# Reordering the opening loads and the opening TensorE jobs of a fused local-attention and squared-ReLU kernel

## The chip, the cores and the metric

The kernel runs on one core of one Trainium2 chip. The metric is the device time of one execution in microseconds (us); lower is better. A comparison of two kernels is made on medians of several executions.

## The reference, cut to what matters

Attention over 4 batches, 8 heads, 768 positions and 64 channels, with a window of 96 positions behind the query and 8 global positions, a distance penalty for each head, and then a two-layer network with a squared ReLU over the 3072 resulting rows.

```python
scores = scale * np.matmul(q, k.transpose(0, 1, 3, 2))
keep = is_global | is_local
scores = np.where(keep, scores - slopes[:, None, None] * dist, -1e9)
a = softmax(scores)
x = np.matmul(a, v)          # -> 3072 rows of 512
h = np.maximum(x @ w_in, 0.0)          # 512 -> 2048
out = h * h @ w_out                    # 2048 -> 512
```

## The kernel before, in words

**Tiling.** A batch has six tiles of 128 rows; a *half* is three tiles, so there are eight halves (`halves[0]` to `halves[7]`, called x0, x1, ...). A query tile meets two key blocks: its own tile, and the block before it, in which the global keys replace the first 32 rows (`kb` for keys, `vb` for values). All work on a half is: load q, k, v; turn q and k so that the 64 channels lie on the partitions; scores; exponentials; weights times v; division by the row sum; turn the result into `xt`; first layer with `w_in_sb`; ReLU and square into `h2`; second layer with `w_out_sb`; store.

**Two regimes.** From the third half on, the attention of the next half is merged into the two dense layers of the present one, so TensorE has always dense work between the small matmuls. The first two halves (batch 0) have no dense work to hide behind. They are handled tile by tile by an *opening*: a list of job names written out by hand, `OPENING`. Its jobs are:

- `T r`: eight TensorE transposes of q and k of tile r (`turn_tile`), two copies out of PSUM, and for inner tiles the `kb` copies.
- `S r o`, `S r b`: scores of tile r with its own block, or with the block before (`score_tile`). For tiles 0 to 2 the distance penalty is added by eight more matmuls; for tiles 3 to 5 the exponentials are multiplied by a mask on VectorE. Two exponentials on ScalarE follow each.
- `V r`: the copies for `vb` (`fix_v`). `A r i`: weights times v for four heads (`attend_tile`), then reciprocal and product on VectorE (`norm`). `X r i`: two transposes into `xt` (`tile_to_x`).
- `F c`, `G c i`: first layer of x0 with quarter c of `w_in`, for tile 0 and for tiles 1 and 2. `E c i`, `D c`: the same for x1, tiles 3 and 4, and tile 5.

After the opening come the rest of the first layer of x1, and the second layer of x0, whose first matmul (line 606) marks the end of the opening in the trace.

**What sets the order.** The program is recorded by a class `Plan`. TensorE jobs stand in one queue and loads in another, each in the order in which they were listed; all other operations are picked by the plan's own costs and due times. The plan then emits everything in that order, and each engine runs its queue strictly in order. Where the plan sees TensorE idle early on, it fills with matmuls on zeros (`warm`, lines 207 and 210), half as many as the idle time holds in the first 5 us. PSUM is given out in rings: `big` has six buffers (transposes of q and k, scores, layers), `att` two (weights times v, and the transposes into `xt`).

**Loads.** All q, k, v tiles but the first q and k, and all weights, are issued by GpSimd (`plan.load`, line 95), which converts fp32 to fp16 on the way. q and k of tile 0 come as fp32 through SyncE and ScalarE (`rsq`, `rsk`, line 330) and are converted by copies. Before any load GpSimd fills two index tables (`fill_index`, lines 227 and 229), on which the identity `ident` (line 233), the mask and all warm transposes rest. The loads were listed as: k1 q1 v0, k2 q2 v1, v2; two quarters of `w_in`; k3 q3 v3, k4 q4 v4, k5 q5 v5; two quarters of `w_in`; four quarters of `w_out`.

Of the kernel before, what the change touches and what calls it, by code (L numbers as in the profile page):

```python
# [8 lines left out]
FP32 = mybir.dt.float32  # L9
# [4 lines left out]
P = 128  # L14
# [2 lines left out]

OPENING = """T0 T1 S0o S1o A00 T2 A01 S1b S2o X01 X00 S2b A10 V1 A11 F0 A20 V2 X10 F1 A21 X20 T3 X11 V3  # L20
X21 S3b S3o T4 G10 G00 T5 S4b A31 A30 S4o G01 G11 G21 X31 S5b A40 G20 X30 S5o A41 V4 G31 G30
X41 X40 F3 A50 A51 E10 F2 E01 X51 E11 X50 E00 D0 D1"""


class Op:
    def __init__(self, costs, emit, needs, rank=0, lag=0.0, land=None, slots=()):
        self.costs, self.emit, self.rank, self.lag, self.land = costs, emit, rank, lag, land
        self.needs = [n for n in needs if n is not None]
        self.slots = slots
        self.done = None  # L30
        self.wait = 0.0
# [17 lines left out]
class Plan:  # L49
# [10 lines left out]
    def __init__(self, warm_from, warm_until):  # L60
        self.warm_from, self.warm_until = warm_from, warm_until
        self.queues = {"PE": [], "LOAD": []}
        self.rest = []
        self.free = {}
        self.landed = 4.4
        self.rank = 0

    def pe(self, cost, emit, needs=(), takes=(), lag=0.24):
# [23 lines left out]
        self.rest.append(op)  # L92
        return op

    def load(self, dur, emit, needs=(), rank=None):
        rank = self.rank + 0.5 if rank is None else rank
        op = Op({"POOL": 0.88}, emit, needs, rank, 0.7, land=dur)
        self.queues["LOAD"].append(op)
        return op

# [8 lines left out]
    def run(self):  # L109
        order = []  # L110
        while self.rest or any(self.queues.values()):
            best = None
            for op in [q[0] for q in self.queues.values() if q] + self.rest:
                r = self.ready(op)
                if r is None:
                    continue
                e = min(op.costs, key=lambda e: max(r, self.free.get(e, 0.0)) + op.costs[e])
                c = (max(r, self.free.get(e, 0.0)), op.rank, e, op)
                if best is None or c[:2] < best[:2]:
                    best = c  # L120
            start, _, e, op = best
            end = start + op.costs[e]
            idle = self.free.get(e, self.warm_from)
            self.free[e] = end
            op.done = end + op.lag
            if op.land is not None:
                self.landed = max(end + 0.8, self.landed) + op.land
                op.done = self.landed + op.lag
            for q in self.queues.values():
                if q and q[0] is op:  # L130
                    q.pop(0)
                    break
            else:
                self.rest.remove(op)
            self.spare = 0.0
            if e == "PE" and start < self.warm_until and op.users:
                self.spare = start - 0.1 - max([idle] + [n.done for n in op.frees])
                self.spare *= 0.5 if start < self.warm_from + 5.0 else 1.0
            op.emit(e)
            order.append((start, end, e, op))  # L140
        return order
# [3 lines left out]
def kernel(  # L145
# [11 lines left out]
    nc = tc.nc  # L157

    B, H, S, D = q.shape
# [7 lines left out]
    HT = HALF // P  # L167
# [9 lines left out]
    stage_p = ctx.enter_context(tc.tile_pool(name="stage", bufs=2))  # L177
# [8 lines left out]
    plan = Plan(1.0, 24.0)  # L186
# [5 lines left out]
    def copy(e, out, in_):  # L192
        if e == "ACT":
            nc.scalar.copy(out=out, in_=in_)  # L194
        else:
            eng(e).tensor_copy(out=out, in_=in_)  # L196
# [24 lines left out]
    w_in_sb = const.tile([P, NCT, d_ff], FP16, name="w_in_sb")  # L221
# [51 lines left out]
    batches = [Batch() for _ in range(B)]  # L273
    halves = [Half() for _ in range(NHB)]
    for hb, x in enumerate(halves):
        x.hb, x.b, x.half = hb, hb // 2, hb % 2
        x.bt = batches[x.b]
    w_in_op, w_out_op = [], []

    def new_batch(bt):  # L280
        bt.qk = qk_p.tile([P, 2, NT, NPAIR, P], FP16, name="qk", tag="qk")
# [9 lines left out]
    def staged(x, name):  # L291
        if getattr(x, name, None) is None:
            setattr(x, name, stage_p.tile([P, HT, H, D], FP16, name=name, tag=name))
        return getattr(x, name)

    def list_loads(x):
        r0 = x.half * HALF
        prev = halves[x.hb - 2] if x.hb >= 2 else None
        before = (prev.turned if prev else []) + (halves[x.hb - 1].turned if x.hb > 3 else [])
        vbefore = [halves[x.hb - x.half - 3].attended[-1]] if x.hb >= 4 else []  # L300

        def rows(src, name, t):
            def emit(e):
                dst = (x.bt.v[:, x.half * HT + t, :, 0:D] if name == "v"
                       else staged(x, name)[:, t, :, :])
                dma = nc.gpsimd.dma_start(out=dst, in_=src[x.b, :, r0 + t * P:r0 + (t + 1) * P, :]  # L306
                                          .rearrange("h p d -> p h d"))
                if x.hb > 3 and name == "sq" and t == 0:
                    for turn in halves[x.hb - 1].turns:
                        behind(dma, turn)  # L310
                if name == "sk":
                    x.last_load = dma
            return plan.load(0.85, emit, vbefore if name == "v" else before)

        if x.half == 0:
            def start(e):
                new_batch(x.bt)
                nc.vector.memset(x.bt.v[:, :, :, D:D + 1], 1.0)
            x.bt.op = plan.add({"DVE": 0.1}, start, vbefore, rank=0)
        if x.hb > 1:  # L320
            x.q_in = [rows(q, "sq", t) for t in range(HT)]
            x.k_in = [rows(k, "sk", t) for t in range(HT)]
            x.v_in = [rows(v, "v", t) for t in range(HT)]
        elif x.hb == 1:
            x.k_in, x.q_in, x.v_in = zip(*((rows(k, "sk", t), rows(q, "sq", t), rows(v, "v", t))
                                           for t in range(HT)))
        else:
            def first(dst, src, eng, e, lag):
                raw = stage_p.tile([P, H, D], FP32, name="r" + dst, tag="r" + dst, bufs=1)
                op = plan.add({e: 0.5}, lambda e: eng.dma_start(  # L330
                    out=raw, in_=src[0, :, 0:P, :].rearrange("h p d -> p h d")), rank=-1)
                op.lag = lag

                def emit(e):
                    copy(e, staged(x, dst)[:, 0], raw)
                return plan.add({"DVE": 0.42, "ACT": 0.54}, emit, [op], rank=0)
            x.k_in = [first("sk", k, nc.scalar, "ACT", 4.1)]
            x.q_in = [first("sq", q, nc.sync, "SP", 3.4)]
            x.v_in = []
            for t in range(1, HT):  # L340
                x.k_in.append(rows(k, "sk", t))
                x.q_in.append(rows(q, "sq", t))
                x.v_in.append(rows(v, "v", t - 1))
            x.v_in.append(rows(v, "v", HT - 1))
        for l in x.v_in:
            l.needs.append(x.bt.op)
        x.bt.v_in = [*getattr(x.bt, "v_in", []), *x.v_in]

    def list_w_in(cs):
        n = d_ff // 4  # L350
        for c in cs:
            w_in_op.append(plan.load(2.65, lambda e, c=c: nc.gpsimd.dma_start(  # L352
                out=w_in_sb[:, :, c * n:(c + 1) * n],
                in_=moe_w_in[:, c * n:(c + 1) * n].rearrange("(k p) f -> p k f", p=P))))

    def list_w_out():
        n = NFT // 4
        for c in range(4):
            w_out_op.append(plan.load(2.65, lambda e, c=c: nc.gpsimd.dma_start(
                out=w_out_sb[:, c * n:(c + 1) * n, :],  # L360
                in_=moe_w_out[c * n * P:(c + 1) * n * P, :].rearrange("(m p) d -> p m d", p=P))))

# [435 lines left out]
    x0, x1 = halves[0], halves[1]  # L798
    tile_ops, kb_ops, tiles = {}, {}, {}
    for bt in batches:  # L800
# [2 lines left out]
    zero_op = plan.add({"DVE": 0.2}, lambda e: nc.vector.memset(zero, 0.0), rank=-3)  # L803
    index = plan.add({"POOL": 0.5}, fill_index, rank=-2)
    list_loads(x0)
    ident_op = plan.add({"DVE": 0.25}, fill_ident, [index], rank=0)
    dist_op = plan.add({"DVE": 2.4}, fill_dist, [ident_op], rank=0)
    slope_ops = [plan.add({"DVE": 0.2}, fill_dist16, [dist_op], rank=0)]
    slope_ops += [plan.add({"ACT": 0.3, "DVE": 0.18}, lambda e, h=h: fill_slope_id(e, h), [ident_op],
                           rank=0) for h in range(H)]  # L810
    mask_ops = [plan.add({"ACT": 0.43}, lambda e, h=h: fill_mask(h), [dist_op], rank=10 + h)
                for h in range(H)]
    list_w_in((0, 1))
    list_loads(x1)
    list_w_in((2, 3))
    list_w_out()

    jobs = {}
# [8 lines left out]
    for c in range(4):  # L827
# [3 lines left out]
        for i in range(2):  # L831
            jobs[f"G{c}{i}"] = lambda ms=ms, i=i: layer1(x0, ms[2 * i:2 * i + 2], P, HALF)
            jobs[f"E{c}{i}"] = lambda ms=ms, i=i: layer1(x1, ms[2 * i:2 * i + 2], 0, 2 * P)
    for name in OPENING.split():
        jobs[name]()
    for job in l1(x1, 8) + l2(x0)[:6]:
        job()
    for hb in range(1, NHB):
        x = halves[hb]
# [51 lines left out]
```

## Time and profile before

| | us |
|---|---|
| median of 6 runs (lowest to highest) | 221.12 (220.59 to 221.75) |
| the profiled execution | 220.91 |
| its span in the profile | 219.1 |
| TensorE busy in the span | 211.5 (96%) |
| ScalarE busy | 128.0 (58%) |
| VectorE busy | 117.2 (54%) |
| GpSimd busy | 68.2 (31%) |

The span is what the profile covers from the first to the last instruction; 1.8 us of the execution lie around it. Busy time of TensorE includes the matmuls on zeros, and matmuls overlap in the pipeline, so a share of 96% is not 96% useful work. Times inside the trace are counted from the start of the span.

### The profile page before, as it was taken

To read this page: it belongs to the slowest core of one execution; us is meant where nothing else is said; L and a number is where in the kernel's file an instruction comes from. 1 tells how busy PE (TensorE), PEld (TensorE's weight loads), DVE (VectorE), ACT (ScalarE), POOL (GpSimd) and SP (SyncE) were. 2 spreads that over 40 slices of the span, in tenths; PEclk is the share of its full clock that TensorE was granted. 3 is DMA by queue.
4 is the path that set the end of the run, shared out by engine and by line. 5 is a ranking of instruction groups with operands and counts; after the bars stand their busy time and mean duration, and the time that the engine had idled before them with its cause. 6 is when DMAs were issued, how large, how long until landed. Compare 5 with 4: busy or idle time off the path is not lost.

```text
span 219.1 us, 4865 instructions
## 1 busy us (share of the span) xinstructions
PE 211.5 (96%) x1928; PEld 128.5 (59%) x1928; DVE 117.2 (54%) x336; ACT 128.0 (58%) x289; POOL 68.2 (31%) x84
## 2 busy tenths in 40 slices
PE   6989899999999999999999999999999999999993
PEld 6767789855555556445654565446554565455552
DVE  7476788433764298606963388407850479104300
ACT  7796897653753779119841688139831786137421
POOL 8986824485058049003900094000000000000000
PEclk9999999999999999999999999999999999999999
DMA  8999999999989959956994999964103101220012
GB/s 122 148 194 157 188 207 207 163 152 142 167 164 155 206 125 154 159 127 139 129 120 112 212 73 151 117 135 106 39 19 114 52 18 39 66 96 0 3 48 95
DMA packets 106727, 26.41 MB, mean 120 GB/s; under 512 B 99408, under 2 KB 103760, under 8 KB 106704
## 3 DMA queue, kind: packets, MB, share of 16 engines
q0 software_dynamic: 77024, 13.37, 87.5%
q1 hardware_dynamic: 28640, 12.46, 23.5%
q10 hardware_dynamic: 1040, 0.26, 0.6%
q8 instruction: 15, 0.25, 0.5%
q14 instruction: 8, 0.07, 0.1%
HBM read 27.26 MB, written 6.29 MB: 153 GB/s over the span
## 4 chain that ended last, share of the span: by engine, by line
PE 76%; DMA 9%; POOL 9%; DVE 2%; ACT 1%; issue 1%; SPq 0%; POOLq 0%
PE hps L557 35%; PE yps L606 30%; DMA v<-in_v_dram 7%; PE av L502 4%; PE sp L447 3%; POOL sk L306 3%; POOL sq L306 3%; POOL v L306 2%; DMA qk<-sk 2%; PE yps L634 2%; PE av L734 1%; POOL w_in_sb L352 1%; ACT qk L194 1%; ACT ex L462 1%; PE sp L695 1%
## 5 line engine op out<-in xcount | busy, mean ns | idle before, releaser
L557 PE MATMUL hps<-xt,w_in_sb 128*128 128x384 f16 (+2 forms) x608 | 89.3, 301 | 0.0
L606 PE MATMUL yps<-w_out_sb,h 128*128 128x512 f16 x368 | 83.0, 379 | 0.0
L557 PEld LDWEIGHTS <-w_in_sb 128*128 128x128 f16 x608 | 53.7, 98 | 26.8 <-DMA w_in_sb<-in_moe_w_in_dram 0.4
L581 ACT ACTIVATE hr<-hps 128x384 f16<-128x384 f32 (+1 forms) x108 | 55.0, 518 | 16.0 <-PE hps L557 13.5
L592 DVE TENSOR_TENSOR h<-hr 128x768 f16<-128x768 f16 (+1 forms) x70 | 36.1, 522 | 52.0 <-ACT hr L581 51.4
L606 PEld LDWEIGHTS <-h 128*128 128x128 f16 x368 | 35.1, 98 | 39.5
L194 ACT COPY y<-yps 128x512 f32<-128x512 f32 (+1 forms) x25 | 14.3, 570 | 59.5 <-PE yps L606 56.9
L462 ACT ACTIVATE ex<-sp 128x384 f16<-128x384 f32 x96 | 36.7, 476 | 2.2 <-PE sp L447 2.1
L306 POOL DMA_DIRECT2D sq<-in_q_dram x23 | 20.4, 893 | 53.8 <-DMA qk<-sq 30.6
L306 POOL DMA_DIRECT2D sk<-in_k_dram x23 | 20.7, 916 | 7.3 <-DVE ph L716 3.6
L306 POOL DMA_DIRECT2D v<-in_v_dram x24 | 21.6, 929 | 3.4 <-DMA w_out_sb<-in_moe_w_out_dram 3.3
L196 DVE COPY vb<-v 128x520 f16<-128x520 f16 (+1 forms) x32 | 10.1, 321 | 9.7 <-DMA v<-in_v_dram 9.2
L511 DVE TENSOR_TENSOR tm<-av,rec 128x384 f16<-128x384 f32 x24 | 13.4, 557 | 0.8
L196 DVE COPY kb<-qk 128x96 f16<-128x96 f16 (+4 forms) x56 | 11.0, 302 | 5.1 <-ACT qk L194 4.2
L502 PEld LDWEIGHTS <-phat 128*128 128x128 f16 x264 | 10.0, 98 | 3.9 <-DVE phat L478 0.7
L478 DVE TENSOR_TENSOR phat<-ex,mask 128x768 f16<-128x768 f16 x24 | 12.2, 549 | 0.0
L502 PE MATMUL av<-v,phat 128*128 128x65 f16 x168 | 11.5, 194 | 0.1
L509 DVE RECIPROCAL rec<-av 128x6 f32<-128x6 f32 x24 | 4.7, 196 | 12.4 <-PE av L502 12.1
L474 DVE TENSOR_TENSOR phat<-ex,mask 128x768 f16<-128x768 f16 (+1 forms) x24 | 10.6, 485 | 0.1
L502 PE MATMUL av<-vb,phat 128*128 128x65 f16 x96 | 10.2, 194 | 0.3 <-DVE phat L478 0.3
L194 ACT COPY qk<-trp 128x512 f16<-128x512 f16 (+1 forms) x14 | 7.5, 562 | 4.9 <-DVE qk L196 2.7
L447 PE MATMUL sp<-qk 64*128 64x128 f16 x168 | 8.9, 219 | 0.0
(67 smaller groups left out, 138.0 us busy)
## 6 DMA issues: line engine op xcount, KB each, us to landing
out_dram<-y SPq DMA_DIRECT2D x23, 256.0 KB, 2.2
v<-in_v_dram POOLq DMA_DIRECT2D x24, 128.0 KB, 6.6
sk<-in_k_dram POOLq DMA_DIRECT2D x23, 128.0 KB, 5.8
sq<-in_q_dram POOLq DMA_DIRECT2D x23, 128.0 KB, 5.3
w_in_sb<-in_moe_w_in_dram POOLq DMA_DIRECT2D x4, 512.0 KB, 8.5
w_out_sb<-in_moe_w_out_dram POOLq DMA_DIRECT2D x4, 512.0 KB, 14.8
xt<-tm SPq DMA_TRANSPOSE x20, 2.9
rsk<-in_k_dram ACTq DMA_DIRECT2D x1, 256.0 KB, 4.7
```

Of the source, the lines that this page charges most:

```text
L194: nc.scalar.copy(out=out, in_=in_)
L196: eng(e).tensor_copy(out=out, in_=in_)
L306: dma = nc.gpsimd.dma_start(out=dst, in_=src[x.b, :, r0 + t * P:r0 + (t + 1) * P, :] .rearrange("h p d -> p h d"))
L447: nc.tensor.matmul(pair[h][:, i * P:(i + 1) * P], lhsT=lhsT, rhs=bt.qk[rows, 0, r, a, :], start=True, stop=True)
L462: nc.scalar.activation(out=st["ex", g][:, h, 0:n], in_=st[g][h][:, 0:n], func=AF.Exp, scale=scale)
L478: eng(e).tensor_tensor(out=phat[:, :, c0:c0 + n].rearrange("p e (i c) -> p e i c", c=P), in0=ex[:, :, 0:n].rearrange("p e (i c) -> p e i c ...
L502: nc.tensor.matmul(av[:, h, j, :], lhsT=phat[:, h, c * P:(c + 1) * P], rhs=rhs, start=n == 0, stop=n == len(mine) - 1)
L511: nc.vector.tensor_tensor(out=st["tm"].rearrange("p t e d -> p e t d"), in0=av[:, :, :, 0:D], in1=rec[:, :, :, None].to_broadcast([P, 2, H ...
L557: nc.tensor.matmul(st["ps"][:, i * n:(i + 1) * n], lhsT=w_in_sb[:, kk, m * P:(m + 1) * P], rhs=x.xt[:, kk, c0:c1], start=kk == 0, stop=kk ...
L581: nc.scalar.activation(out=o, in_=i, func=AF.Relu)
L592: eng(e).tensor_tensor(out=x.h2[:, m0:m0 + width, c0:c1], in0=hr, in1=hr, op=ALU.mult)
L606: nc.tensor.matmul(st["ps"], lhsT=x.h2[:, m, j * P:(j + 1) * P], rhs=w_out_sb[:, m, :], start=m == 0, stop=m == NFT - 1)
```

## The change

`OPENING` is replaced by another order, and the opening loads get an order of their own, `LOADING`: q and k of tiles 1 to 5 and v of tiles 0 to 2 stand ahead of the first quarter of `w_in`; v3, v4 and v5 stand between and behind the quarters. The first of these loads (k of tile 1) has rank -3, ahead of the index tables (rank -2), so GpSimd issues it first. The rest changes the plan's own costs and due times (they decide what is picked next and how many matmuls on zeros are put in), not the operations. In the built program GpSimd's queue begins: load k1, iota, iota, q1, k2, q2, k3, v0, q3, v1, q4, k4, v2, k5, q5, c0, v3, c1, v4, c2, c3, v5, then four quarters of `w_out` (cN is quarter N of `w_in`). The matmuls on zeros are 40 ahead of T0, 14 ahead of T1, 4 ahead of T2 and 1 later: 59, where there were 36, 18 and 14 more: 68. VectorE converts k of tile 0 and ScalarE q of tile 0; before, VectorE did both. From the second layer of x0 on, TensorE's order is the same.

```diff
-OPENING = """T0 T1 S0o S1o A00 T2 A01 S1b S2o X01 X00 S2b A10 V1 A11 F0 A20 V2 X10 F1 A21 X20 T3 X11 V3
-X21 S3b S3o T4 G10 G00 T5 S4b A31 A30 S4o G01 G11 G21 X31 S5b A40 G20 X30 S5o A41 V4 G31 G30
-X41 X40 F3 A50 A51 E10 F2 E01 X51 E11 X50 E00 D0 D1"""
+OPENING = """T0 T1 S0o T2 S1o S2o A00 A01 S1b X00 S2b T3 V4 A10 A11 S3o V1 T4 A21 X01 S3b X11 V3 A20 X21
+S4o X10 X20 S4b T5 G01 V2 A30 F0 G00 S5b F1 X30 S5o G10 A40 A41 G11 G21 G20 X40 G30 A31 X41
+F3 X31 A51 G31 A50 E11 X51 E10 X50 E00 D0 D1 E01 F2"""
+LOADING = """k1 q1 k2 q2 k3 v0 q3 v1 q4 k4 v2 k5 q5 c0 v3 c1 v4 c2 c3 v5"""
...
-        self.free = {}
-        self.landed = 4.4
+        self.free = {e: 0.75 for e in ("ACT", "DVE", "POOL", "SP")}
+        self.landed = 3.4
...
-    def load(self, dur, emit, needs=(), rank=None):
+    def load(self, dur, emit, needs=(), rank=None, lag=2.6):
         rank = self.rank + 0.5 if rank is None else rank
-        op = Op({"POOL": 0.88}, emit, needs, rank, 0.7, land=dur)
+        op = Op({"POOL": 0.92}, emit, needs, rank, lag, land=dur)
...
-                self.landed = max(end + 0.8, self.landed) + op.land
+                self.landed = max(end + 1.45, self.landed) + op.land
...
+            for t in range(HT):
+                r = x.half * HT + t
+                if r > 0:
+                    for src, name, key, ops in ((k, "sk", "k", x.k_in), (q, "sq", "q", x.q_in)):
+                        load_jobs[f"{key}{r}"] = lambda src=src, name=name, ops=ops, t=t: (
+                            ops.__setitem__(t, rows(src, name, t, -3 if not plan.queues["LOAD"]
+                                                    else None)))
+                load_jobs[f"v{r}"] = lambda t=t: (
+                    x.v_in.__setitem__(t, rows(v, "v", t)), x.v_in[t].needs.append(x.bt.op))
...
     list_loads(x0)
+    list_loads(x1)
+    for c in range(4):
+        load_jobs[f"c{c}"] = lambda c=c: load_w_in(c)
+    x0.k_in[0] = first_tile(x0, "sk", k, nc.scalar, "ACT", 3.8)
+    x0.q_in[0] = first_tile(x0, "sq", q, nc.sync, "SP", 3.4)
+    for name in LOADING.split():
+        load_jobs[name]()
...
-    dist_op = plan.add({"DVE": 2.4}, fill_dist, [ident_op], rank=0)
+    dist_op = plan.add({"DVE": 2.1}, fill_dist, [ident_op], rank=0)
...
-    list_w_in((0, 1))
-    list_loads(x1)
-    list_w_in((2, 3))
     list_w_out()
```

## The prediction, made before the changed kernel ran

> **What bounds the kernel now.** I read the clock and span first, then the busy time by stretches, the waits, TensorE's timeline of the opening, and the transfers. The stretches (time, TensorE busy, weight loads, VectorE, ScalarE, GpSimd, clock, share of the DMA engines, GB/s):
>
> ```profile
> 0.00:5.50 5.50, 3.83 (x36) 3.83 (x36) 4.04 (x17) 4.24 (x12) 4.74 (x11) 1.00 0.85 122
> 5.50:8.50 3.00, 2.73 (x37) 2.44 (x36) 1.28 (x2) 1.81 (x6) 3.00 (x4) 1.00 2.35 149
> 8.50:16.00 7.50, 6.62 (x124) 5.29 (x121) 5.00 (x15) 6.90 (x16) 6.66 (x9) 1.00 1.54 179
> 16.00:25.00 9.00, 8.06 (x121) 6.27 (x118) 5.70 (x21) 6.25 (x14) 6.38 (x9) 1.00 2.25 163
> 25.00:47.00 22.00, 22.00 (x277) 18.14 (x278) 15.81 (x47) 17.89 (x36) 10.70 (x14) 1.00 1.66 188
> ```
>
> From 25 us on TensorE is never idle, and the chain of waits runs along its layer matmuls to the end. So only the time before 25 us can be won, and what is won there is won for the whole, as long as the data of later halves are there. The timeline shows what ends the last waits (start, length, ..., idle time before and its releaser):
>
> ```profile
> 1.67 4.00 PE L210 MATMUL trp<-ident,zero 128*128 128x128 f16 x36 [1.67 <-DVE ident L233]
> 5.54 0.61 PE L662 MATMUL trp<-ident,sq 128*128 128x128 f16 x4
> ...
> 6.82 1.39 PE L210 MATMUL trp<-ident,zero 128*128 128x128 f16 x18
> ...
> 14.11 0.40 PE L761 MATMUL trx<-ident,tm 128*128 128x128 f16 x4 [0.61 <-DVE tm L746]
> ...
> 19.66 0.40 PE L662 MATMUL trp<-ident,sq 128*128 128x128 f16 x4 [0.24 <-DMA sq<-in_q_dram]
> ...
> 22.37 0.40 PE L662 MATMUL trp<-ident,sq 128*128 128x128 f16 x4 [0.46 <-DMA sq<-in_q_dram]
> ...
> 24.95 0.40 PE L662 MATMUL trp<-ident,sq 128*128 128x128 f16 x4 [0.21 <-ACT qk L194]
> ```
>
> T3, T4 and T5 each start when q of their tile lands: the transfers' view gives issue plus time to landing as 10.16 + 9.4, 12.75 + 9.6 and 18.32 + 6.6 us, that is 19.6, 22.3 and 24.9. They stand behind two quarters of `w_in`, which landed at 7.81 + 7.3 = 15.1 and 17.7. Not dense work between T0's end (6.82) and the second layer's start (46.80), from the timeline's starts: zeros 1.23, 0.45, 0.23, 0.42; waits 0.61, 0.27, 0.46, 0.21; zeros with a wait 0.64 (ahead of T3) and 0.96 (ahead of S3). Sum 5.48 us. Useful work there is 46.80 - 6.82 - 5.48 = **34.5 us**, and the change leaves it alone.
>
> **What the Trainium skill says.** *TensorE: Matmul & The Clock Gate*, "What's actually happening": 1.2 GHz until a free-running window of about 3.4 us was busy, then 2.4. The trace agrees: transposes stand 107 ns apart until 7.24 us and 56 ns after, 5.6 us after the first one. *GPSIMD Engine Reference*, "1. Specifications": GpSimd shares its SBUF interface with VectorE, and VectorE instructions in a two-port mode or with two SBUF inputs contend. The trace agrees for copies: one `vb` pair took 1.52 us while a v load was being issued (11.45 us) and 0.60 us between issues (14.70 us). *DMA: Bandwidth & Descriptors*, "Specifications": line rate needs at least 512 B. The page here counts 99408 of 106727 packets below that; a tile lands 0.89 us after the last one, four times its bytes of `w_in` 2.6 us after.
>
> **The change, part by part.**
>
> *1. Load k1 ahead of the iotas.* GpSimd's first load takes 1.10 us:
>
> ```profile
> 0.84 0.34 POOL L227 IOTA dist<- 128x256 f32 x1 [0.39 <-POOLq L872]
> 1.14 0.13 POOL L229 IOTA pidx<- 128x1 f32 x1
> 1.39 1.10 POOL L306 DMA_DIRECT2D sk<-in_k_dram  x1
> 2.48 0.89 POOL L306 DMA_DIRECT2D sq<-in_q_dram  x1
> ```
>
> k1 can go at 0.75, when ScalarE and SyncE issue theirs, so it lands at about 6.1 instead of 6.8; nothing needs it so early, since q1 is issued at 2.4 as before and lands at 7.7. The price: `ident` comes 1.10 us later (1.21 to 2.31), and TensorE's first zero at 2.77. Forty zeros at 107 ns take 4.27: **T0 from 7.05 to 7.91 instead of 5.54 to 6.82, a loss of 1.1 us.** The converted q0 and k0 (rsq at 4.8, rsk at 5.4, then a copy of 0.65 to 0.90 each, now on two engines) are ready by about 6.4 and no longer set T0. Behind T0's copy on ScalarE stand five masks at 0.43 us, in order, so the exponentials of S0 start at 8.1 + 0.5 + 2.1 = 10.7 (before 9.63). A clock that warms before 7 us gives back up to 0.8 of this, one that warms at 9.6 adds 0.8 (window bounds: 2.77 + 3.4 and 2.77 + 6.8); I take the middle, with T1 at 8.7.
>
> *2. q and k ahead of the weights.* From q1 at 7.7, 0.89 us for each tile: q2 9.4, q3 12.1, q4 13.9, q5 17.4. T3 to T5 stand at 15, 17 and 21 us in the walk below, so no transposes wait for q any more. **This removes the three DMA waits and the zeros put before them: 0.64 + 0.96 + 0.46 + 0.21 = 2.3 us.** The first quarter of weights lands at 17.4 + 2.6 = 20.0 (before 15.1), then v3 20.9, c1 23.5, v4 24.4, c2 27.0, c3 29.6, v5 30.5. At most eight loads are in flight (k5 is issued when `w_in` lands); by that rule c0 waits for v0 (11.2) and c3 for v2: no gap.
>
> *3. The new order.* TensorE has no first-layer work before 20.0. From T0's end, with job lengths from the timeline (T 0.45, S 0.87 with penalty and 0.33 without, A 0.19 or 0.30, X 0.11, F 0.90, G 0.87):
> - Zeros 0.78 ahead of T1, 0.22 ahead of T2 (no wait hides them).
> - S2o waits 0.3 for the copy of T2, which stands between exponentials on ScalarE (two of 0.5 us for each S); A10 waits 0.5 for the exponentials of S1b.
> - A21 to X20 (17.5 to 22 us) come close together: the `att` ring has two buffers, each given back by a reciprocal and product of 0.55 us on VectorE or a copy of 0.38 on ScalarE. Walking it: X01, X11, X21, X10 wait 0.44, 0.47, 0.35, 0.47; G01 waits 0.29 for the copy of X20 and starts at 21.9, 1.9 after its weights.
> - From there F1 stands at 25.2 (c1 23.5), G21 at 28.0 (c2 27.0), G30 at 30.7 (c3 29.6), A51 at 33.1 (v5 30.5): dense.
>
> Sum of not dense time after T0: 0.78 + 0.22 + 0.3 + 0.5 + 1.73 + 0.29 = 3.8 us.
>
> *4. Plan costs, copies on other engines, ring use:* nothing of their own; they are in the order walked above. A kb or vb copy beside a load issue can take 0.9 us more (second page cited); VectorE has room for that except at 17 to 21 us, when GpSimd is on weights, which take it fewer issues: 0 to 0.6 us, taken as 0.
>
> **Sum:** second layer at 7.91 + 34.5 + 3.8 = 46.2 instead of 46.80: **-0.6 us**. After it nothing takes this back: tile loads of the third half landed at 47.3 and are used at 51.98; the last `w_out` at 41.7 and used about 49.4. The profiled execution would go from 220.91 (span 219.1 and 1.8 around it) to 220.3; it lay 0.21 below the median, so I say 220.5.
>
> **Rivals.** *Late start wins (slower).* The three DMA waits go, but the later `ident` moves T0, its copy, the masks and every exponential behind them; ScalarE is nearly full from 10.7 to 24 us and cannot catch up. With the clock at 9.6 us (+0.8) and contended copies in the `att` stretch (+0.6), the sum is +0.8: 221.9. Of the 1.7 us of holes that go (5.48 - 3.8), 1.1 are already spent on T0, so it decides as soon as 0.6 us more is lost there. For it: ScalarE is 6.90 of 7.50 us busy from 8.5 to 16. Against: between 16 and 25 us it still had 2.75 of 9 us idle before.
>
> *Weights late.* Transfers slip 0.5 to 1.5 us (c3 took 3.8 us after c2 in the trace before, issued back to back): G30 then waits up to 1.1, which eats the gain: about 221.3. Against: 1.0 us or more of room at every quarter.
>
> *Early clock, shorter holes (clearly faster).* The clock warms before 7 us, one case in four of the window's phase, and the `att` waits come out half: -0.8 - 0.6 more: 219.4 to 219.8. That the change does not do what it says is excluded by the built order, told above.
>
> **How the numbers follow.** As walked 0.50 (own range 219.8 to 221.2), clearly faster 0.21, weights late 0.09, late start 0.20. A measurement of this kernel tells about 0.3% (0.66 us) from no change, and 220.5 lies at that edge: the first case gives 0.22 faster, 0.26 same and 0.02 slower, the second 0.21 faster, the third 0.07 same and 0.02 slower, the last 0.02 same and 0.18 slower: 0.43, 0.35 and 0.22. Range 219.3 to 221.9: it leaves out the far half of the late start (0.10) and some 0.07 of the tails of the others.
>
> **What would show it.** Right: `ident` near 2.3, first T0 transpose near 7, no wait on sq or sk on TensorE, first hps at 21 to 22.5, `trx` and `av` waiting for VectorE between 17 and 22, second layer near 46.2. Wrong: waits of hps on `w_in_sb`, a first hps after 23, idle TensorE between 25 and 46, or a second layer beyond 46.8.

## The result, and the profile after

| | before | after |
|---|---|---|
| median, us (runs; lowest to highest) | 221.09 (40; 220.15 to 222.53) | 219.36 (19; 218.81 to 220.88) |
| ratio, with its interval of 95% | | 0.9928 (0.991 to 0.9945) |
| the profiled execution, its span | 220.91, 219.1 | 219.3, 217.5 |
| second layer starts | 46.80 | 46.03 |
| from there to the end of the last matmul | 168.87 | 168.00 |

The kernel became 1.7 us faster: the sign forecast, but nearly three times the 0.6 us of the likeliest case, and only 0.06 us inside the fast end of the range. The last two rows say why. In this pair of profiles 0.77 us came from the opening, and 0.87 from a place behind it, of which the forecast knew nothing.

**The opening.** The same stretches as in the prediction, now of the kernel after (time, TensorE busy, weight loads, VectorE, ScalarE, GpSimd, clock, share of the DMA engines, GB/s):

```profile
0.00:5.50 5.50, 2.46 (x24) 2.57 (x25) 3.18 (x14) 3.41 (x10) 4.37 (x11) 1.00 0.94 129
5.50:8.50 3.00, 3.00 (x39) 3.00 (x37) 1.48 (x3) 1.34 (x3) 3.00 (x4) 1.00 2.18 139
8.50:16.00 7.50, 7.23 (x132) 5.89 (x129) 4.70 (x15) 7.50 (x17) 7.22 (x9) 1.00 2.30 146
16.00:25.00 9.00, 8.07 (x135) 6.33 (x133) 8.51 (x30) 8.71 (x20) 5.74 (x8) 1.00 1.48 187
25.00:47.00 22.00, 21.97 (x264) 18.04 (x258) 14.06 (x42) 15.93 (x31) 11.34 (x14) 1.00 1.68 187
```

ScalarE now has next to nothing left from 8.5 to 25 us (7.50 of 7.50 and 8.71 of 9 us busy), nor has VectorE from 16 on (8.51 of 9): most attention of batch 0 is crowded there. TensorE's timeline of the opening (start, length, ..., idle time before and its releaser):

```profile
3.04 4.43 PE L214 MATMUL trp<-ident,zero 128*128 128x128 f16 x40 [3.04 <-DVE ident L237]
7.26 0.53 PE L668 MATMUL trp<-ident,sq 128*128 128x128 f16 x4
...
14.78 0.40 PE L668 MATMUL trp<-ident,sq 128*128 128x128 f16 x4
...
15.88 0.57 PE L740 MATMUL av<-v,ph 128*128 128x65 f16 x13 [0.27 <-ACT ph L714]
...
18.76 0.27 PE L767 MATMUL trx<-ident,tm 128*128 128x128 f16 x2 [0.29 <-ACT xt L198]
...
20.79 0.28 PE L767 MATMUL trx<-ident,tm 128*128 128x128 f16 x2 [0.22 <-DVE tm L752]
...
21.34 0.40 PE L668 MATMUL trp<-ident,sq 128*128 128x128 f16 x4
...
21.79 1.04 PE L563 MATMUL hps<-xt,w_in_sb 128*128 128x256 f16 x8
```

T0 starts at 7.26 instead of 5.54. T3, T4 and T5 stand at 14.78, 16.70 and 21.34 (before 19.66, 22.37 and 24.95) and no longer wait for q; what waits there are the small jobs of the `att` ring, for copies and products. The first layer starts at 21.79. The transfers' view shows the exchange: tiles of q in the first 40 us land 6.3 us after their issue (before 9.5), quarters of `w_in` 10.1 (before 8.5).

**The second gain, at 77 to 79 us.** VectorE's timeline of the kernel before, and TensorE's at the same place:

```profile
75.01 0.61 DVE L196 COPY vb<-v 128x520 f16<-128x520 f16 x2 [4.07 <-DMA v<-in_v_dram]
76.05 0.61 DVE L196 COPY vb<-v 128x520 f16<-128x520 f16 x2 [0.42 <-DMA v<-in_v_dram]
76.59 0.54 DVE L592 TENSOR_TENSOR h<-hr 128x768 f16<-128x768 f16 x1
77.06 0.54 DVE L583 TENSOR_SCALAR hr<-hps 128x384 f16<-128x384 f32 x1
77.53 1.00 DVE L478 TENSOR_TENSOR phat<-ex,mask 128x768 f16<-128x768 f16 x2
```

```profile
77.26 0.34 PE L447 MATMUL sp<-qk 64*128 64x128 f16 x6
77.65 0.34 PE L447 MATMUL sp<-qk,kb 64*128 64x128 f16 x6
78.12 0.20 PE L502 MATMUL av<-v,phat 128*128 128x65 f16 x1
78.59 0.20 PE L502 MATMUL av<-vb,phat 128*128 128x65 f16 x1 [0.26 <-DVE phat L478]
```

VectorE stood for 4.07 us with a `vb` copy at the head of its queue whose v had not landed. Square (`h`), ReLU (`hr`) and mask (`phat`) are behind it in order, so ReLU comes at 77.06 and the mask at 77.53, and TensorE's `av`, which needs the mask, stands. In the kernel after, VectorE and then TensorE:

```profile
73.97 0.56 DVE L598 TENSOR_TENSOR h<-hr 128x768 f16<-128x768 f16 x1 [2.33 <-ACT hr L587]
74.64 0.56 DVE L589 TENSOR_SCALAR hr<-hps 128x384 f16<-128x384 f32 x1
75.12 0.60 DVE L200 COPY vb<-v 128x520 f16<-128x520 f16 x2
75.65 1.01 DVE L484 TENSOR_TENSOR phat<-ex,mask 128x768 f16<-128x768 f16 x2
```

```profile
76.49 0.34 PE L453 MATMUL sp<-qk 64*128 64x128 f16 x6
76.67 0.33 PE L453 MATMUL sp<-qk,kb 64*128 64x128 f16 x6
76.93 0.20 PE L508 MATMUL av<-v,phat 128*128 128x65 f16 x1
76.97 0.20 PE L508 MATMUL av<-vb,phat 128*128 128x65 f16 x1
```

Square and ReLU stand ahead of the only `vb` pair there, the other pair has moved behind these masks (to 84.84 us), and `phat` comes at 75.65. From the first scores (`sp`) to the second `av` TensorE took 1.33 us before (77.26 to 78.59) and 0.48 after: 0.85 of the 0.87 us lie at this one place. The window of 77 to 79 us shows only a part of them as idle, since the few small matmuls there count as busy until their modelled end. The windows of 77 to 79 us, before and then after (TensorE 1.56 us busy against 2.00):

```profile
77.00:79.00 2.00, 1.56 (x27) 0.90 (x26) 2.00 (x6) 1.84 (x6) 0.00 (x0) 1.00 1.04 256
```

```profile
77.00:79.00 2.00, 2.00 (x23) 1.35 (x24) 1.97 (x6) 2.00 (x7) 0.00 (x0) 1.00 0.77 173
```

The list of waits had the sum in one line, before and then after (engine, line, waited for: us in total, times, longest):

```profile
DVE vb L196 <- DMA v<-in_v_dram: 9.2, 7, 4.1
```

```profile
DVE vb L200 <- DMA v<-in_v_dram: 0.9, 2, 0.6
```

### The profile page after: what moved, and what is told of

Same layout as the page of the kernel before. It is cut to its first block, busy times and chain, and to the rows that moved or that the text cites. A ratio compares the mean times of both kernels' runs of the same rounds, so it can differ in the third digit from the quotient of the medians.

```text
span 217.5 us, 4853 instructions
## 1 busy us (share of the span) xinstructions
PE 209.8 (96%) x1919; PEld 127.8 (59%) x1919; DVE 118.4 (54%) x337; ACT 127.3 (59%) x288; POOL 68.1 (31%) x84
## 4 chain that ended last, share of the span: by engine, by line
PE 91%; ACT 5%; DVE 2%; POOL 1%; issue 0%; POOLq 0%
PE hps L563 39%; PE yps L612 37%; PE sp L453 5%; PE av L508 4%; ACT ph L714 2%; PE trp L214 2%; PE yps L640 2%; ACT mask L269 1%; ACT qk L198 1%; PE av L740 1%; PE trp L400 1%; PE trx L767 1%; PE trp L668 1%; POOL sk L310 0%; PE sp L701 0%
## 5 line engine op out<-in xcount | busy, mean ns | idle before, releaser
L310 POOL DMA_DIRECT2D sq<-in_q_dram x23 | 20.4, 895 | 52.3 <-DMA qk<-sq 29.2
L200 DVE COPY kb<-qk 128x96 f16<-128x96 f16 (+4 forms) x56 | 11.7, 288 | 1.0 <-ACT qk L198 0.9
L480 DVE TENSOR_TENSOR phat<-ex,mask 128x768 f16<-128x768 f16 (+1 forms) x24 | 10.7, 485 | 0.1
L214 PE MATMUL trp<-ident,zero 128*128 128x128 f16 x58 | 5.8, 282 | 3.0 <-DVE ident L237 3.0
## 6 DMA issues: line engine op xcount, KB each, us to landing
w_in_sb<-in_moe_w_in_dram POOLq DMA_DIRECT2D x4, 512.0 KB, 10.1
```

## The experiments

The theory after the first comparison: two separate gains, the opening (some 0.8 us) and the wait of TensorE at 77 to 79 us that hangs on VectorE's `vb` copy (some 0.9). The rivals: the opening alone won 1.7 and the wait goes with it; the plan's costs won it; the late T0 still costs 1.1 and hides a larger gain. Kernels derived from before begin with b_, those from after with a_; costs_only has both old orders. Ratios are to the kernel before, measured again in the same round, with their intervals; they are not exactly the ratio of the two medians. The mean clock is the share of TensorE's full clock that was granted, averaged over one execution.

**b_vb_late: the late vb copy alone.** In the kernel before, the plan holds the `vb` copies of the third batch back longer; nothing up to the second layer is moved. With the pair the plan moved one `xt` copy and some ReLUs on VectorE and ScalarE, all of them behind 72 us.

```diff
-                      wait=0.0 if bt is batches[0] else 4.0)
+                      wait=0.0 if bt is batches[0] else 8.0 if bt is batches[2] else 4.0)
```

> The kernel before, with one number changed: the vb copies of the third batch get a due time of 8 us after their data instead of 4. TensorE, GpSimd and SyncE keep their order; on VectorE one of two vb pairs ahead of the masking at 75 us moves behind it. Theory (the second half of the gain, 0.86 us, was a wait of weights-times-v at 77 to 79 us behind a vb copy at the head of VectorE's queue): the wait goes, about 220.2, 0.8 to 0.9 us below the kernel before, with the opening unchanged (second layer near 46.8). Rival (the wait came from v landing late, or all of the gain is the opening's): no change, within 0.2 us.

Measured: 220.63 us (22 runs), ratio 0.9992 (0.9974 to 1.001). VectorE's timeline:

```profile
75.30 0.56 DVE L592 TENSOR_TENSOR h<-hr 128x768 f16<-128x768 f16 x1 [2.33 <-ACT hr L581]
75.78 0.60 DVE L196 COPY vb<-v 128x520 f16<-128x520 f16 x2
76.45 1.03 DVE L478 TENSOR_TENSOR phat<-ex,mask 128x768 f16<-128x768 f16 x2
```

The wait is gone (168.00 us from the second layer to the end, where before had 168.87), as the theory says. But the second layer began at 47.37 in this profile, 0.57 later than in that of before, with the same opening, so a part of the wait could have gone without the edit. By the medians the gain is 0.4 us, half of the 0.8 to 0.9 expected, with an interval that reaches no change.

**a_vb_early: the copy put back into the kernel after.**

```diff
-                      wait=0.0 if bt is batches[0] else 4.0)
+                      wait=0.0 if bt is batches[0] else 1.0 if bt is batches[2] else 4.0)
```

> The changed kernel, with the due time of the third batch's vb copies at 1 us instead of 4, so that both pairs stand ahead of the masking at 75 us on VectorE, as in the kernel before. Theory: the wait of weights-times-v comes back, 0.8 to 1.2 us slower than the changed kernel (TensorE is earlier against the same loads), about 220.3, that is 0.6 to 0.9 us below the kernel before. Rival (all of the gain is the opening's): as fast as the changed kernel, about 219.4.

Measured: 220.26 us (22 runs), ratio 0.9968 (0.9947 to 0.9989), 0.9 us above after. (In four runs the mean clock was 0.990 to 0.992; the median of the 18 others is 220.02, 0.7 above after.) VectorE, then TensorE:

```profile
74.53 0.62 DVE L200 COPY vb<-v 128x520 f16<-128x520 f16 x2 [0.67 <-DMA v<-in_v_dram]
75.08 0.54 DVE L598 TENSOR_TENSOR h<-hr 128x768 f16<-128x768 f16 x1
```

```profile
77.08 0.20 PE L508 MATMUL av<-vb,phat 128*128 128x65 f16 x1 [0.24 <-DVE phat L484]
```

The wait is back, 0.41 us long in this profile (168.41). So some 0.7 to 0.9 of the 1.7 us hang, in the medians, on one copy's place in VectorE's queue.

**Which part of the change moves it?** Three kernels that each lack something:

a_old_loads keeps all of after but the old order of loads:

```diff
-LOADING = """k1 q1 k2 q2 k3 v0 q3 v1 q4 k4 v2 k5 q5 c0 v3 c1 v4 c2 c3 v5"""
+LOADING = """k1 q1 v0 k2 q2 v1 v2 c0 c1 k3 q3 v3 k4 q4 v4 k5 q5 v5 c2 c3"""
```

> The changed kernel with the new TensorE order but the loads listed as before (two quarters of w_in ahead of k3, q3 and the rest; k1 still ahead of the iotas). Theory (order and loads belong together: q and k ahead of the weights is what lets T3 to T5 go early): T3 waits for q3 near 19.6 instead of starting at 14.8, T5 near 25; with first-layer jobs listed behind T5 TensorE idles or runs zeros for some 5 us before that: second layer at 49 to 51, 4 to 5 us slower than the changed kernel, about 223.5 to 224.5. Rival (the new TensorE order alone brings the gain): within 0.5 us of the changed kernel.

Measured: 227.51 us (6 runs), ratio 1.0318 (1.028 to 1.0355); T3 at 21.2, the first layer at 30.08 us, the second at 55.66. It was worse than expected by 3 to 4 us: q of tiles 3 to 5 lands behind the weights as before, but the new order has no first layer to do meanwhile, and 77 zeros stand ahead of T3. The clock also fell for a while (mean 0.990 to 0.992 in four of the six runs; the two others took 226.52 and 227.1 us).

a_old_jobs keeps all but the old order of TensorE jobs:

```diff
-OPENING = """T0 T1 S0o T2 S1o S2o A00 A01 S1b X00 S2b T3 V4 A10 A11 S3o V1 T4 A21 X01 S3b X11 V3 A20 X21
...
+OPENING = """T0 T1 S0o S1o A00 T2 A01 S1b S2o X01 X00 S2b A10 V1 A11 F0 A20 V2 X10 F1 A21 X20 T3 X11 V3
...
```

> The kernel after with its new order of loads, but with the old order of TensorE jobs. The first layer's F0 stands ahead of T3 there, and its weights land at 20.9 instead of 15.1, those of F1 at 24.5; TensorE works in order, so everything behind F0 stands. F1 started at 17.8 us before; from 24.5 on the rest follows as before without the three waits for q (2.1 us): second layer at 46.8 + 6.7 - 2.1 = 51.4 and 225 to 226 us. Rival: the plan's costs and the earlier q and k make up for it, and the order of jobs is of little weight: 220 to 222.

Measured: 224.84 us (6 runs), ratio 1.0147 (1.0105 to 1.019), second layer at 51.12 where 51.4 was worked out. TensorE's timeline, at F0 (21.21 us, behind 25 zeros) and F1; their weights now land at 20.3 and 23.7 us:

```profile
15.82 5.56 PE L211 MATMUL hps<-zero 128*128 128x512 f16 x25
...
23.74 1.07 PE L563 MATMUL hps<-xt,w_in_sb 128*128 128x128 f16 x16 [1.11 <-DMA w_in_sb<-in_moe_w_in_dram]
```

costs_only has the two edits above together and, by this one, the iotas first; the plan's new costs and due times stay.

```diff
-                            ops.__setitem__(t, rows(src, name, t, -3 if not plan.queues["LOAD"]
-                                                    else None)))
+                            ops.__setitem__(t, rows(src, name, t)))
```

> The kernel after with the old order of loads, the old order of TensorE jobs and the iotas first; what stays is the plan's changed costs, lags and due times, with the zeros and the copies' engines that they choose. Theory: the gain of the opening comes from loads and jobs, and the gain at 77 to 79 us from the vb copy, which stands ahead of the masks again here: 221.0 (220.6 to 221.4), second layer near 46.8, VectorE waiting for v at about 75 us. Rival: the costs by themselves bring part of it: 219.8 to 220.4.

Measured: 221.15 us (22 runs), ratio 0.9994 (0.9974 to 1.0014). VectorE's timeline:

```profile
75.69 0.61 DVE L200 COPY vb<-v 128x520 f16<-128x520 f16 x2 [1.39 <-DMA v<-in_v_dram]
76.81 0.61 DVE L200 COPY vb<-v 128x520 f16<-128x520 f16 x2 [0.51 <-DMA v<-in_v_dram]
```

The costs alone bring nothing. Either order alone costs 3.5 to 6.5 us against before; only together they win. (Both new orders with the old costs were not run, so whether the new costs are needed too stays open.) In all three kernels both `vb` pairs stand ahead of the mask that waited, in the built order of VectorE; with both new orders one pair moves. So the second gain comes of the plan's choosing anew after both lists changed, not of an edit made at that place. The second layer of costs_only began at 48.69 in its profile, later than the 46.8 expected, since T4 waited 1.57 us for q (24.41), and yet TensorE did not wait at 77 to 79 us (168.00): v had landed only 0.76 later than in before, TensorE came 1.89 later.

**a_z30_vb_early: is that wait of fixed length?** It has the early copy of a_vb_early and ten zeros less ahead of T0.

```diff
+            if r == 0:
+                plan.spare = 30.5 * (128 / 2400 + 0.003)
             warm(trp.rearrange("p i a c -> p (i a c)"))
...
+                      wait=0.0 if bt is batches[0] else 1.0 if bt is batches[2] else 4.0)
```

> The kernel after with two edits together: 30 zeros ahead of T0 (which alone brought the second layer from 46.03 to 45.56) and the early vb copy of a_vb_early (which alone left 168.41 us from the second layer to the end of TensorE instead of 168.00). If v of that half lands at a time that TensorE's start does not move, the wait grows by what the opening wins: about 168.8 from the second layer to the end, and the time of a_vb_early, 220.2. The rival, a wait of fixed length: 168.4, and 219.8.

Measured: 220.9 us (14 runs), ratio 0.9974 (0.9944 to 1.0004), which leaves out the two slowest runs: no faster than a_vb_early, though its opening starts earlier. (In four runs the mean clock was 0.989 to 0.992; the median of the ten others is 220.3.) VectorE's timeline, then TensorE's:

```profile
74.53 0.61 DVE L200 COPY vb<-v 128x520 f16<-128x520 f16 x2 [3.38 <-DMA v<-in_v_dram]
75.54 0.61 DVE L200 COPY vb<-v 128x520 f16<-128x520 f16 x2 [0.39 <-DMA v<-in_v_dram]
```

```profile
77.14 0.34 PE L453 MATMUL sp<-qk,kb 64*128 64x128 f16 x6 [0.80 <-DVE hr L589]
```

From the second layer (45.54) to the end it took 169.61 us, a wait of 1.61, more than either theory said, because v came 1.0 us later than in a_vb_early. The first TensorE job to stand is not `av` but a score job, 0.80 us, for the ReLU (`hr`) that stands behind the copies on VectorE and gives a PSUM buffer back; the masks follow it. So everything that VectorE has behind the copy holds TensorE. It is a floor: with the copy early, TensorE cannot pass that place before v has landed and been copied. Setting its level by a_vb_early alone (last copy's start 74.53, second layer 45.73, wait 0.41, so 28.39 us lie between without a wait), the wait is *last copy's start - second layer - 28.39*:

| kernel with the early copy | last copy starts | second layer | worked out | measured |
|---|---|---|---|---|
| before | 76.05 | 46.80 | 0.86 | 0.87 |
| a_z30_vb_early | 75.54 | 45.54 | 1.61 | 1.61 |
| costs_only | 76.81 | 48.69 | none (-0.27) | 0.00 |

In the other kernels told of here but a_vb_early the same distance was 168.00 to 168.04 us. And in all 14 profiled executions the time, less the second layer's start and less this wait, is 173.24 to 173.29 us: to within 0.05 us the kernels differ in these two terms alone.

**b_vb_late_again and after_again: the corners once more.** No edits of their own; both ran on one chip.

> The kernel before with the late vb copy once more, on the same chip and in the same rounds as the kernel after: a second profile of the old opening that is free of the wait at 77 to 79 us. If the opening alone won 0.8 us, as the first pair of profiles shows, its median lies 0.8 above that of after_again; if the old opening is usually later than in that profile, as the first run of this edit suggests (47.37), it lies 1.2 to 1.3 above. 168.0 us from the second layer to the end in both.

> The kernel after once more: 219.4 us, second layer between 45.7 and 46.5, 168.0 us from there to the end. With the runs of the kernel before, b_vb_late_again and a_vb_early it gives the four corners of old or new opening and early or late vb copy.

Measured: 220.67 us (14 runs), ratio 0.9983 (0.996 to 1.0005), and 219.46 (13 runs), ratio 0.9946 (0.9922 to 0.997). The second layer began at 48.16 and 46.06, with 168.00 us behind it in both. Medians in us:

| | early vb copy | late vb copy |
|---|---|---|
| old opening | 221.09, 221.01, 221.3, 221.03 (before) | 220.63, 220.67 |
| new opening | 220.26 | 219.36, 219.46 (after) |

In these medians the new opening is worth 1.2 to 1.3 us where nothing waits for v. Against before as measured in the same round, it is worth 0.8 where something does wait, and the late copy 0.4 on the old opening (its intervals reach no change); on the new one the late copy is worth 0.9. (With the runs of a fallen clock left out, 0.8 becomes 0.9 and 0.9 becomes 0.7.) A floor would do this: each gain is whole only with the other. But the intervals are some 0.4 us wide to either side, so the medians alone do not show that the two gains depend on each other; the table of profiles above does. In b_vb_late_again TensorE waited in the opening for these:

```profile
15.57 1.07 PE L557 MATMUL hps<-xt,w_in_sb 128*128 128x128 f16 x16 [0.61 <-DMA w_in_sb<-in_moe_w_in_dram]
...
18.14 1.07 PE L557 MATMUL hps<-xt,w_in_sb 128*128 128x128 f16 x16 [0.93 <-DMA w_in_sb<-in_moe_w_in_dram]
...
23.78 0.40 PE L662 MATMUL trp<-ident,sq 128*128 128x128 f16 x4 [1.47 <-DMA sq<-in_q_dram]
```

The old opening started the second layer at 46.80, 47.37 and 48.16 in three profiles, as q and weights happened to land; the new one at 46.03, 46.06 and 45.73 (a_vb_early). The prediction had the earliest of the old ones before it. By the 173.26 us behind the start, a median of 220.65 without the wait means a start at 47.4, one of 219.4 a start at 46.1: by the medians the opening won 1.2 to 1.3 us and the wait was some 0.4, where the first pair of profiles had 0.77 and 0.87.

**a_iota_first and a_iota_fill: what the late T0 costs.** The first puts the iotas ahead of k1 again (first edit); the second has zeros ahead of S3o and S3b besides (second edit, in `score_tile`).

```diff
-                            ops.__setitem__(t, rows(src, name, t, -3 if not plan.queues["LOAD"]
-                                                    else None)))
+                            ops.__setitem__(t, rows(src, name, t)))
```

```diff
+            more = {(3, False): 3, (3, True): 2}.get((r, bool(before)), 0)
+            plan.spare = max(plan.spare, 0.0) + more * (512 / 2400 + 0.003)
             warm(pair[0].rearrange("p a c -> p (a c)"))
```

> The changed kernel, but GpSimd issues its index iotas ahead of the first load, as in the kernel before (40 zeros ahead of T0, 13 ahead of T1). Theory (the late identity is a loss, hidden in the sum): identity near 1.3 instead of 2.8, T0's end near 6.6 to 6.8 instead of 7.8, the exponentials and the att stretch behind it 0.7 to 1.0 us earlier, second layer near 45.2; 218.6. Rival (the loads or the att ring set the pace): second layer unchanged near 46.0, about 219.4, or slower where the later k1 holds T1.

Measured: 220.6 us (14 runs), ratio 0.9973 (0.9947 to 0.9999), slower than after. T0 began at 5.89, 1.37 earlier, but T4 at 16.37 (after 16.70) and T5 at 21.48 (after 21.34): S3o waits 0.86 us for a copy on ScalarE, and the ring's waits grow. And the clock fell, 1.06 us ahead of T5. TensorE in windows of 3.4 us:

```profile
17.00:20.40 3.40, 2.10 (x38) 1.24 (x34) 3.23 (x11) 2.81 (x8) 2.70 (x4) 1.00 1.40 169
20.40:23.80 3.40, 3.40 (x29) 2.58 (x28) 2.88 (x10) 3.00 (x7) 1.49 (x2) 0.50 1.51 193
```

After a window with 2.10 us of work the clock is at half for the next. Ten of the 14 runs had a mean clock of 0.982 to 0.992; the four others (0.999 and 1.00) took 218.36 to 219.55.

> The kernel after with its iotas ahead of k1, and with three matmuls on zeros more ahead of S3o and two more ahead of S3b, that is 1.07 us of work in holes in which TensorE waits anyway. Theory: with the iotas first the fall of TensorE's clock to half from 20.4 to 23.9 us came from the 3.4 us before it, in which TensorE was busy for 2.10 us only; with the holes filled (some 2.5 to 2.9 us busy) the clock stays, the mean clock is 1.00 in most runs instead of 0.991, and the time is 219.2 instead of 220.6. Rival 1: the fall has nothing to do with the holes: 220.6 to 221, clock 0.991 as before. Rival 2: the zeros are in the way: 219.6 to 220.0 at clock 1.00.

Measured: 219.2 us (6 runs), ratio 0.9896 (0.9857 to 0.9934), all six at a mean clock of 0.998 or above:

```profile
17.00:20.40 3.40, 2.47 (x40) 1.36 (x36) 3.23 (x11) 2.81 (x8) 2.71 (x4) 1.00 1.50 186
20.40:23.80 3.40, 3.40 (x56) 3.06 (x55) 3.08 (x11) 3.40 (x9) 1.49 (x2) 1.00 1.54 194
```

So zeros in holes that TensorE waits through anyway took the fall away, 1.4 us. With the clock kept, the iotas' place is worth nothing that can be told: 219.2 against 219.36 and 219.46.

**a_zeros_30 and a_z30_fill: the late T0 alone.** The plan's order stays; ten zeros go (the first edit of a_z30_vb_early). a_z30_fill adds one zero of 512 columns ahead of S3o and of S3b.

```diff
+            more = {(3, False): 1, (3, True): 1}.get((r, bool(before)), 0)
+            plan.spare = max(plan.spare, 0.0) + more * (512 / 2400 + 0.003)
             warm(pair[0].rearrange("p a c -> p (a c)"))
```

> The kernel after with 30 instead of 40 matmuls on zeros ahead of T0 and nothing else moved: the last zero then ends at about 6.25 us, q of tile 0 is converted at 5.3 and k at 6.6, so T0 runs from about 6.3 instead of 7.26. If the late T0 is a loss on the path, as the prediction counted it (1.1 us), the exponentials and all behind come up to 0.9 earlier: the second layer at 45.2 instead of 46.0 and 218.5 us. The rival: what comes after 14 us is set by tiles, copies and exponentials that the earlier T0 does not move in full, so T5 stays near 21.3, the second layer near 46.0, and the time near 219.3.

Measured: 219.28 us (8 runs), ratio 0.9899 (0.9865 to 0.9932). Its timeline:

```profile
6.19 0.39 PE L670 MATMUL trp<-ident,sq 128*128 128x128 f16 x4
...
20.86 0.40 PE L670 MATMUL trp<-ident,sq 128*128 128x128 f16 x4
```

T0 is 1.07 us earlier, T5 0.48, the second layer (45.56) 0.47: half of the lead runs into waits for copies, the first of them 0.35 us ahead of S3o. In the medians nothing of it can be told from after.

> The kernel after with 30 zeros ahead of T0 and one matmul on zeros more (0.22 us) ahead of each of S3o and S3b, where TensorE waited 0.35 and 0.17 to 0.29 us in a_zeros_30. Earlier start and a clock that stays up together: second layer 45.6, clock 1.00 in all runs, 218.9 to 219.2 us. The rival: the zeros delay what they stand ahead of, and nothing is left over the kernel after: 219.4.

Measured: 219.26 us (5 runs), ratio 0.9913 (0.9885 to 0.994), second layer at 46.41. Here c3, the last quarter of `w_in`, landed at 31.16 us, and the first layer stood for it (the line names an earlier releaser, ScalarE, which was long done):

```profile
31.21 1.05 PE L563 MATMUL hps<-xt,w_in_sb 128*128 128x256 f16 x8 [0.79 <-ACT xt L198]
```

In after c3 landed at 30.4, and these matmuls began at 30.64, with 0.24 us to spare. An earlier opening is caught by the weights: no version that was run is measurably better than the kernel after.

## Why the prediction was half right

It had the sign, the holes that go and the order of events in the opening; it had the opening's gain too small, and put at nothing a place behind it. That 219.36 still lay in its range was luck: the range reached down there for another mechanism, the early clock.

**Step 1, the late start: right in time, dear in price.** `ident` came at 2.76 (forecast 2.31, with the first load at 0.75; it went at 1.25), the first zero at 3.04 (2.77), T0 ran 7.26 to 7.84 (7.05 to 7.91), the clock rose at 7.53 us, near the middle that was taken, ScalarE's exponentials began at 11.06 (10.7). But "a loss of 1.1 us" as a loss on the path is not what a_zeros_30 shows (0.47 of 1.07 in the profile), nor a_iota_fill (none). The rival *late start wins*, which rested on it, fell.

**Step 2, q ahead of the weights: right, too small.** T3 to T5 wait for no transfer. The tiles landed as walked up to q3 (12.06 for 12.1), then 0.9 to 1.7 late (q5 18.3 for 17.4; c0 20.9 for 20.0; c3 30.4 for 29.6). The size was low: the "2.3 us" of waits removed are those of one profile. (Of them, 0.96 were zeros ahead of S3, behind T3, and no wait for q.) Another profile of the same opening, b_vb_late_again, has 3.3 us of waits for transfers (0.61 + 0.93 + 0.27 + 1.47). This is the larger part of the miss: the new opening was walked right (46.03 for 46.2), but the old one, at 46.80 in the profile that it was compared with, starts the second layer at some 47.4 in the median, and the opening won 1.2 to 1.3 us where 0.6 was forecast.

**Step 3, the new holes: right in sum.** 46.03 - 7.84 - 34.5 = 3.7 us not dense where 3.8 was walked, the first layer at 21.79 for 21.9, the second at 46.03 for 46.2. The single waits at the ring came out shorter (0.17 to 0.29 in the trace, walked 0.35 to 0.47); the sum agrees better than its items, which is in part luck, and where the rest lies is not resolved.

**Step 4 failed.** "Plan costs, copies on other engines, ring use: nothing of their own" and "From 25 us on TensorE is never idle" were read from the window 25 to 47 and carried to the end. One window more, 77 to 79, shows 1.56 of 2.00 us, and the list of waits had VectorE's 9.2 us for v. A plan that chooses by its own clock chooses anew everywhere when its opening moves; that was looked at for TensorE's queue, which stayed the same, and not for VectorE's. Missed: 0.87 us in the pair of profiles, some 0.4 in the medians. The sum by profiles is -0.77 - 0.87 = -1.64, measured -1.7 in the medians.

**What "nothing takes this back" would have cost.** With the copy left early, 0.8 to 0.9 us is what remains of the opening's gain, and an opening that starts still earlier (a_z30_vb_early) adds nothing to it. That the prediction's figure of -0.6 is near this was luck: it came from the waits of one early profile, not from a floor.

**The rivals.** *Early clock, shorter holes* named a time of 219.4 to 219.8, near what was measured, by a mechanism that did not occur: the clock rose near the middle of its range. *Weights late* did not decide in after, but "1.0 us or more of room at every quarter" was wrong: 0.24 at c3, and a_z30_fill paid 0.79 there.

## What to carry to other kernels

A gain ahead of a long dense stretch is whole only if everything behind it still comes in time: look for transfers at the head of an in-order queue (the list of waits, VectorE for DMA here) to the very end, and compare the built order of every engine, not of the one that was edited. A single profile of a stretch that waits for transfers is one draw: the same opening lay 1.4 us apart in three profiles, and its gain was 0.77 us in the first pair of profiles but 1.2 to 1.3 in the medians. Order of loads and order of jobs are one decision: either alone cost 3.5 to 6.5 us here, both together won 1.7.

## What the hardware showed that was not expected

TensorE's clock can fall back in the middle of a busy opening. *TensorE: Matmul & The Clock Gate*, "What's actually happening", in the Trainium skill gives the throttled state as the one after at least one idle window of about 3.4 us; a_iota_first shows it after a window of that length in which TensorE worked for 2.10 us, and for one window, 20.4 to 23.8 us, at a price of 1.4 us in the median. Busy time does not decide it: b_vb_late_again had 1.53 us of work in the 3.00 us from 21 to 24 and kept its clock in that profile.

The traces say more if the windows are laid where the clock itself changes. In a_iota_first it rises at 6.76, falls at 20.42 and rises again at 23.83 us: 4 and 1 times 3.41 us. Laid in such steps from the first rise of each profile, the windows ahead of the two falls in an opening had 2.12 (a_iota_first) and 1.58 us of work (a_old_loads), but windows with 1.84 (costs_only) and 1.95 (b_vb_late_again) brought no fall. The columns that the matmuls of a window stream, counted half where only 64 rows of the array are used, do sort them: 2570 and 2312 ahead of those two falls, 1536 or fewer ahead of the falls at the end of six profiles, and 3023 or more in every other whole window of the 14 profiles. (At 128 columns in 56 ns a full window would hold some 7800.) So many small matmuls that look busy can be too little work. This count was picked after the fact, and a few records of matmuls may be missing: it is a pattern of these traces, and no run was made to test it.
